# Moving two small softmax steps from VectorE to GpSimd in the attention stage of an attention and mixture-of-experts kernel

## The chip, the cores and the metric

The kernel runs on one core of a Trainium2 chip. The time is the device time of one execution in microseconds (us): the median of three runs is 686.33 us, the lowest 684.86 and the highest 687.82. A core has four compute engines that work side by side and wait for one another by semaphores: TensorE (PE in the profile; its weight loads are PEld), VectorE (DVE), ScalarE (ACT) and GpSimd (POOL). SyncE (SP) only issues transfers here.

## The reference

Three layers follow one another: causal attention with a decay (4 batches, 8 heads, 576 positions, 64 channels), a soft mixture of 8 experts with 4 slots each, and a second mixture of 4 experts that is weighted by given probabilities. The change is in the softmaxes of the middle layer, which the kernel computes during attention.

```python
def _attn_ref(q, k, v, f):
    scores = scale * np.matmul(q, k.transpose(0, 1, 3, 2))
    log_f = np.log(np.clip(f, 0.0001, 1.0))
    cum = np.cumsum(log_f, axis=-1)
    decay = cum[:, :, :, None] - cum[:, :, None, :]
    scores = np.where(causal, -1000000000.0, scores + decay)
    ...softmax over the last axis...
    return np.matmul(attn, v)

def _moe_ref(x, phi, w1, w2):           # x: 2304 tokens x 512
    logits = x @ phi                    # 2304 x 32
    d = np.exp(logits - logits.max(0, keepdims=True))
    d /= d.sum(0, keepdims=True) + 1e-09        # dispatch: over the tokens
    slot_input = (d.T @ x).reshape(E, S_per_e, D)
    for e in range(E):
        slot_out[e] = np.maximum(slot_input[e] @ w1[e], 0.0) @ w2[e]
    c = np.exp(logits - logits.max(1, keepdims=True))
    c /= c.sum(1, keepdims=True) + 1e-09        # combine: over the 32 slots
    return c @ slot_out

def _moe2_ref(x, domain_probs, w1, w2):
    p = domain_probs / (domain_probs.sum(-1, keepdims=True) + 1e-09)
    for e in range(E):
        out += p[:, e:e + 1] * (np.maximum(x @ w1[e], 0.0) @ w2[e])
    return out
```

## The kernel before

**The attention loop.** The 32 (batch, head) combinations are worked in 16 pairs of heads. A pair has seven steps (`STEPS`, `NS` = 7): step 3 does the last block of queries for both heads together, the other six do one block of 128 queries (or two) of one head. In each step `scores` multiplies queries with keys on TensorE; `soft` takes the masked minimum on VectorE (L198, a custom instruction with a second one that reads its result `nm`) and the exponential on ScalarE (L202); two steps later `transposes` turns the exponentials around on TensorE (L249, L258), and ScalarE or VectorE copies them out of PSUM (L168 and L170 are the two arms of the helper `copy`). `av_a` and `av_b` (L276, L288) multiply with the values for the pair before.

**The split of the operands.** Scores use a high and a low part of q and k. `split_a` and `split_b` make them for the heads of the next pair: ScalarE casts q (L168 CAST), GpSimd scales q (L180, which waits until TensorE has read the old operand) and subtracts (L179, which waits for the cast), VectorE casts k (L170 CAST), and GpSimd subtracts (L190). These are GpSimd's main work in attention.

**What is done once in a batch.** When the four pairs of a batch are done, the logits of its 576 tokens lie in `lg`, 128 partitions by 5 chunks by 32 slots. During the first pair of the next batch, `after_tr` calls three pieces of softmax work. At step 2 `dlog` turns the logits (PE L371, L372), finds the dispatch maximum of the tokens so far (`nm`, L377) and takes the exponentials (`dt`, and `al`, the factor for the sums so far, L382). At step 3 `csoft1` takes each token's maximum (`cm`, L350), subtracts it (`ce`, L352) and takes the exponential on ScalarE (L355). At step 4 `dnat` turns `dt` back (L395), `dsum` updates the running maximum `mm[:, 0:1]` and the running sum `ssum` (L387 to L389), and `csoft2` normalizes the combine weights (L360 to L363). At step 6 `sadd` adds to the slot inputs `s_sb` on TensorE (L406, L412) and VectorE (L415); after it `logits` and its PE lines L322 and L324 follow. This happens three times, for batches 0, 1 and 2; the last batch is finished by other code after the loop, which calls `csoft1` too, and there L352 is on GpSimd already.

**What sets the order.** In the loop TensorE's order is fixed by hand (`manual_schedule` for PE). The order on the other engines is found by the framework's scheduler when the kernel is built; each engine then works off its list in order, and each instruction waits for what it needs. Both kernels can be listed engine by engine.

Of the kernel before, what the change touches and what calls it, by code (L numbers as in the profile page):

```python
# [13 lines left out]
ALU = mybir.AluOpType  # L14
# [3 lines left out]
B, H, S, D = 4, 8, 576, 64  # L18
# [16 lines left out]
def soft_moe_kernel(tc, a, out):  # L35
    nc = tc.nc
    pe, dve, act, pool, sp = nc.tensor, nc.vector, nc.scalar, nc.gpsimd, nc.sync
# [10 lines left out]
    with ExitStack() as top:  # L48
# [101 lines left out]
        mm = tl.tile([128, 5], F32, name="mm")  # L150
        warm, ssum = mm[0:1, 4:5], mm[:, 3:4]
# [115 lines left out]
        lt, av, ot, xn, lb = {}, {}, {}, {}, {}  # L267
# [79 lines left out]
        def csoft1(b):  # L347
            lg = lb[b]["lg"]
            cm = sm.tile([128, 5], F32, tag="cm", bufs=1, name=f"cm_{b}")
            dve.tensor_reduce(cm, lg, axis=AX.X, op=ALU.max)  # L350
            ce = wk.tile([128, 5, 32], F32, tag="ce", bufs=1, name=f"ce_{b}")
            (pool if b == B - 1 else dve).tensor_tensor(ce, lg, cm[:, :, None].to_broadcast([128, 5, 32]), op=ALU.subtract)  # L352
            lb[b]["ce"] = ce
            if b < B - 1:
                act.activation(ce, ce, AF.Exp)  # L355
# [28 lines left out]

        def dsum(b):
            al, ds = lb[b]["al"], lb[b]["ds"]
            dve.tensor_scalar(mm[:, 0:1], lb[b]["nm"], -1.0, None, op0=ALU.mult)  # L387
            dve.scalar_tensor_tensor(ssum, ssum, al, ds[:, 0:1], op0=ALU.mult, op1=ALU.add)
            dve.tensor_tensor(ssum, ssum, ds[:, 1:2], op=ALU.add)  # L389

        def dnat(b):
            dt = lb[b]["dt"]
# [52 lines left out]
        def after_tr(g):  # L445
            pr, st = divmod(g, NS)
            pr -= 1
            b = pr // NP - 1
            if st == 5 and 0 <= pr < LASTP and not (pr and pr % NP == 0):
                nat(pr)  # L450
            if st == 0 and pr > 1 and (pr - 1) % NP == 0:
                logits(pr - 1)
            if pr > 0 and pr % NP == 0:
                if st == 2:
                    dlog(b)
                elif st == 3:
                    csoft1(b)
                elif st == 4:
                    dnat(b)
                    dsum(b)  # L460
                    csoft2(b)
# [84 lines left out]
        with tc.manual_schedule(engines={E.PE, E.Activation, E.DVE}):  # L546
# [20 lines left out]
            lg = lb[B - 1]["lg"]  # L567
# [3 lines left out]
            lm = scr[:, 130:162]  # L571
            dve.tensor_reduce(lm, lg[:, 0:4].rearrange("p c s -> p s c"), axis=AX.X, op=ALU.max)
            csoft1(B - 1)
            pe.transpose(mt[:, 128:192], lg[:64, 4], ident[:64, :64])
            pe.transpose(mt[:, 0:128], lm, ident)
# [6 lines left out]
            nm = sm.tile([128, 1], F32, tag="dm", bufs=1, name="dm_e")  # L582
            dve.tensor_reduce(nm[:32], mm[:32, 0:2], axis=AX.X, op=ALU.max, negate=True)
            ds = sm.tile([128, 2], F32, tag="ds", bufs=1, name="ds_e")
            dt = wk.tile([128, S], F32, tag="dt", name="dt_e")
            act.activation(dt[:32], tr, AF.Exp, bias=nm[:32], accum_out=ds[:32, 0:1])
            al = sm.tile([128, 1], F32, tag="al", bufs=1, name="al_e")
# [18 lines left out]
            ce = lb[B - 1]["ce"]  # L606
# [166 lines left out]
        for e in range(E1 - 2):  # L773
# [18 lines left out]
            if e == 5:  # L792
# [14 lines left out]
                for jq in range(4):  # L807
                    for i in range(2):
# [3 lines left out]
                                           op1=ALU.mult)  # L812
# [419 lines left out]
```

## Time and profile before

| quantity | before |
|---|---|
| median of three runs | 686.33 us (684.86 to 687.82) |
| the profiled execution, its own time | 686.2 us |
| its span | 684.4 us |
| PE busy | 664.2 us (97% of the span) |
| DVE busy | 505.4 us (74%) |
| POOL busy | 415.2 us (61%) |
| ACT busy | 342.2 us (50%) |

The span is the time from the first to the last instruction that the profile holds; 1.8 us of the execution lie around it. Attention takes about the first 228 us. The three stretches in which the once-a-batch work runs begin at about 73, 126 and 178 us; they look alike to a few hundredths of a microsecond, so the rows below are of the first, and the others are named where it matters. The mean of a group over the whole span says little about them.

### The profile page before, as it was taken

Reading aid. Unit: us, or ns where it says so; the run is one execution under the profiler, and the core shown is the slowest. Engines: PE = TensorE matmul, PEld = TensorE weight load, DVE = VectorE, ACT = ScalarE, POOL = GpSimd, SP = SyncE. Lnnn points to the kernel's source line nnn. Section 1 sums busy time; section 2 is a strip of 40 time slices with the busy share of each in tenths; the row PEclk is TensorE's granted clock in tenths of the full one; section 3 lists DMA queues with packets and bytes.
Section 4 is the critical chain, followed back from the end, with each engine's and each line's share of the span. In section 5 each row is a group of like instructions: output and inputs, shape, how many; then the busy total and the mean of one; then the engine's idle time right before and its main releaser. Section 6 shows DMA issues by size and latency. Waiting matters only on the chain.

```text
span 684.4 us, 15289 instructions
## 1 busy us (share of the span) xinstructions
PE 664.2 (97%) x5642; PEld 584.1 (85%) x5642; DVE 505.4 (74%) x1370; ACT 342.2 (50%) x817; POOL 415.2 (61%) x377
## 2 busy tenths in 40 slices
PE   6999999999999999999999999999999999999997
PEld 3777677677677545999999999999999999999997
DVE  7888987998996302976777976777976777977764
ACT  4767666766664103633455534455534355544441
POOL 5677656657652126953589934589934589935442
PEclk8899999999999999999999999999999999999999
DMA  6587778723325896031100112100212100001111
GB/s 191 174 263 246 240 228 270 225 76 108 107 56 216 333 417 258 1 124 56 70 1 1 73 53 68 57 1 1 85 41 82 43 2 1 32 33 62 47 47 62
DMA packets 27138, 76.15 MB, mean 111 GB/s; under 512 B 3772, under 2 KB 4156, under 8 KB 27064
## 3 DMA queue, kind: packets, MB, share of 16 engines
q1 hardware_dynamic: 27064, 75.18, 32.1%
q8 instruction: 45, 0.74, 0.5%
q14 instruction: 29, 0.24, 0.1%
HBM read 70.31 MB, written 4.72 MB: 110 GB/s over the span
## 4 chain that ended last, share of the span: by engine, by line
PE 88%; DVE 8%; issue 2%; ACT 1%; SPq 1%; DMA 1%; POOL 0%; DVEq 0%; ACTq 0%
PE R L1022 27%; PE Q L1022 13%; PE P L1022 7%; PE avb L276 5%; PE pt L258 5%; PE two L835 5%; PE d L1042 3%; PE sc L228 3%; PE sc L212 3%; PE sc L227 2%; PE two L731 2%; PE pl L324 2%; PE ava L288 2%; PE so_ps L755 2%; PE pt L249 2%
## 5 line engine op out<-in xcount | busy, mean ns | idle before, releaser
L901 POOL TENSOR_TENSOR s<-S,s 128x512 fp32r<-128x512 f32 x136 | 174.3, 1316 | 137.8 <-ACT s L897 137.8
L897 ACT CAST s<-S 128x512 fp32r<-128x512 f32 x136 | 75.0, 619 | 86.1 <-DVE S L893 75.9
L202 ACT ACTIVATE p<-p,nm 128x256 f32<-128x256 f32 (+2 forms) x144 | 83.4, 580 | 49.8 <-DVE nm L198 49.3
L1022 PE MATMUL R<-wh_T,s 128*128 128x256 f32 x544 | 87.2, 282 | 0.5 <-DVE acc L1005 0.4
L1005 DVE SCALAR_TENSOR_TENSOR acc<-R,dpn,acc 128x256 f32<-128x256 f32 x115 | 55.5, 482 | 38.9 <-PE R L1022 37.1
L867 ACT ACTIVATE a<-two 128x256 f32<-128x256 f32 x68 | 26.1, 383 | 98.8 <-PE two L835 95.2
L1022 PEld LDWEIGHTS R<-wh_T,s 128*128 128x128 f32 x544 | 74.4, 190 | 1.0 <-ACT a L876 1.0
L198 DVE CUSTOM_DVE_ANT_0 p<-sc,maskb 128x256 f32<-128x256 f32 (+2 forms) x144 | 66.1, 488 | 3.9 <-PE sc L212 0.9
L893 DVE SCALAR_TENSOR_TENSOR S<-two,S 128x256 f32<-128x256 f32 x136 | 57.1, 420 | 3.0 <-POOL s L901 0.2
L893 DVE SCALAR_TENSOR_TENSOR S<-two,a 128x256 f32<-128x256 f32 x136 | 56.3, 414 | 0.0
L179 POOL TENSOR_TENSOR opd<-raw,opd 64x576 fp32r<-64x576 f32 x30 | 44.6, 1486 | 13.7 <-ACT opd L168 12.3
L258 PE MATMUL pt<-ident,p 128*128 128x128 f32 x288 | 47.7, 285 | 4.6 <-ACT ptb L168 2.5
L190 POOL TENSOR_TENSOR opd<-raw,opd 64x576 fp32r<-64x576 f32 x31 | 44.0, 1421 | 10.8 <-DVE opd L170 9.5
L258 PEld LDWEIGHTS pt<-ident,p 128*128 128x128 f32 x288 | 31.3, 143 | 21.9 <-issue 16.4
L227 PE MATMUL sc<-opd 128*128 128x256 f32 (+3 forms) x128 | 47.5, 381 | 1.0 <-POOL opd L179 1.0
L883 DVE SCALAR_TENSOR_TENSOR q<-two,q 128x512 fp32r<-128x512 f32 x68 | 46.3, 680 | 0.0
L835 PE MATMUL two<-c4t,gs 128*128 128x256 f32 x288 | 45.8, 282 | 0.3 <-ACT gs L168 0.3
L180 POOL TENSOR_SCALAR opd<-raw 64x576 fp32r<-64x576 f32 x30 | 20.5, 683 | 39.9 <-PE sc L228 17.9
L276 PE MATMUL avb<-ptb,v 128*64 128x192 f32 (+3 forms) x384 | 43.9, 348 | 0.4
L1022 PE MATMUL R<-wh_T,q 128*128 128x256 f32 x272 | 44.1, 285 | 0.0
L1022 PE MATMUL Q<-wh_B,s 128*128 128x256 f32 x272 | 43.6, 283 | 0.0
L1022 PE MATMUL R<-wh_B,a 128*128 128x256 f32 x272 | 43.6, 282 | 0.0
(245 smaller groups left out, 1699.6 us busy)
## 6 DMA issues: line engine op xcount, KB each, us to landing
w<-in_w SPq DMA_DIRECT2D x50, 512.0 KB, 5.0
ring<-in_m SPq DMA_DIRECT2D x28, 512.0 KB, 6.1
raw<-in_k SPq DMA_DIRECT2D x64, 144.0 KB, 2.9
v<-in_v SPq DMA_DIRECT2D x16, 320.0 KB, 5.2
out<-acc SPq DMA_DIRECT2D x18, 256.0 KB, 2.0
raw<-in_q SPq DMA_DIRECT2D x15, 288.0 KB, 4.3
ring<-in_w SPq DMA_DIRECT2D x8, 512.0 KB, 4.6
w_opd<-in_w SPq DMA_DIRECT2D x4, 512.0 KB, 5.2
```

The source lines that it names most:

```text
L198: dve.tensor_tensor_reduce(out=pt_in[j][:, k0:k0 + n], in0=sc, in1=maskb[:, m0:m0 + n], scale=-SCALE, scalar=nm, op0=ALU.add, op1=ALU.min, ...
L202: act.activation(p, p, AF.Exp, bias=nm, scale=-1.0, accum_out=sums)
L227: pe.matmul(o, lhsT=qa[hh][:, qs], rhs=ka[hh][:, 0:n], start=True, stop=False)
L258: pe.transpose(t[:, i, :], pt_in[j][:, 128 * i:128 * i + 128], ident)
L276: pe.matmul(t[64 * hh:64 * hh + 64, q0:q1], lhsT=v_raw[pr][:kk, i, 64 * hh:64 * hh + 64], rhs=ptb[2 * pr + hh][:kk, b0:b0 + q1 - q0], star ...
L835: pe.matmul(t[:, j, k], lhsT=gs[e][:, 128 * fc:128 * fc + 128], rhs=c4t[:, nb * BLK:nb * BLK + BLK])
L883: dve.scalar_tensor_tensor(o[:, 1], i, 0.0, f32(o[:, 0]), op0=ALU.max, op1=ALU.subtract)
L893: dve.scalar_tensor_tensor(sv[m, name][:, c], half[m, h][:, :, k, 128 * t:128 * t + 128], 0.0, other, op0=ALU.max, op1=op)
L897: act.copy(tile_of(m, name)[:, 0], sv[m, name])
L901: (eng or pool).tensor_tensor(o[:, 1], sv[m, name], f32(o[:, 0]), op=ALU.subtract)
L1005: dve.scalar_tensor_tensor(o, t, pcol, o, op0=ALU.mult, op1=ALU.add)
L1022: pe.matmul(t, lhsT=a[:, c, :], rhs=w[:, c, :], start=first and x == 0 and c == 0, stop=x == 2 and c == 3, skip_group_check=True)
```

## The change

`csoft1` puts the subtraction of the maximum (L352) on GpSimd for every batch, where before that was so for the last batch only. `dsum` is written anew on GpSimd: the scaling of `nm` stays one instruction, and the update of `ssum`, a scalar_tensor_tensor and a tensor_tensor before, becomes three tensor_tensor instructions, each of one element in a partition. What is computed is the same.

```diff
@@ csoft1
             dve.tensor_reduce(cm, lg, axis=AX.X, op=ALU.max)
             ce = wk.tile([128, 5, 32], F32, tag="ce", bufs=1, name=f"ce_{b}")
-            (pool if b == B - 1 else dve).tensor_tensor(ce, lg, cm[:, :, None].to_broadcast([128, 5, 32]), op=ALU.subtract)
+            pool.tensor_tensor(ce, lg, cm[:, :, None].to_broadcast([128, 5, 32]), op=ALU.subtract)
@@ dsum
             al, ds = lb[b]["al"], lb[b]["ds"]
-            dve.tensor_scalar(mm[:, 0:1], lb[b]["nm"], -1.0, None, op0=ALU.mult)
-            dve.scalar_tensor_tensor(ssum, ssum, al, ds[:, 0:1], op0=ALU.mult, op1=ALU.add)
-            dve.tensor_tensor(ssum, ssum, ds[:, 1:2], op=ALU.add)
+            pool.tensor_scalar(mm[:, 0:1], lb[b]["nm"], -1.0, 1.0, op0=ALU.mult, op1=ALU.mult)
+            for x, op in ((al, ALU.mult), (ds[:, 0:1], ALU.add), (ds[:, 1:2], ALU.add)):
+                pool.tensor_tensor(ssum, ssum, x, op=op)
```

On VectorE the place is the first pair after batch 0, from the maximum `cm` to the copies of the transposed exponentials; a minus marks what the list of before has and that of the change has not. `sc`, `p` and `nm` are scores, exponentials and minima of attention, `dm` is the dispatch maximum, `ptb` a copy of transposed exponentials, and `mm` holds `ssum` in one of its columns.

```order
 L350 TENSOR_REDUCE cm_1102<-lg_448 128x5
 L170 CAST opd_91<-raw 128x576
-L352 TENSOR_TENSOR ce_1104<-lg_448,cm_1102 128x160
 L198 ISA p_126,nm_4_1_1077<-sc_1_1065,maskb,nm_4_0_1075 128x192
 L198 ISA nm_4_1_1077 128x1
-L387 TENSOR_SCALAR mm<-dm_1057 128x1
-L388 SCALAR_TENSOR_TENSOR mm<-mm,al_1062,ds_1047 128x1
-L389 TENSOR_TENSOR mm<-mm,ds_1047 128x1
 L170 COPY ptb_1096<-pt_1095 128x4x128
 L219 COPY rs<-r_5_1074 64x1 x2
```

Four instructions have left VectorE's list, two stretches of it close up, and nothing else on it changes its place.

On GpSimd at the same place the list of before reads as follows; `opd` are the operands of the scores, and the names end in the number of a tile.

```order
L343 TENSOR_SCALAR l_0_974<-lg_448 128x640
L190 TENSOR_TENSOR opd_92<-raw,opd_92 64x576
L180 TENSOR_SCALAR opd_91<-raw 64x576
L179 TENSOR_TENSOR opd_91<-raw,opd_91 64x576
L190 TENSOR_TENSOR opd_91<-raw,opd_91 64x576
L180 TENSOR_SCALAR opd_92<-raw 64x576
L179 TENSOR_TENSOR opd_92<-raw,opd_92 64x576
```

The list of the change, from the same instruction on:

```order
L343 TENSOR_SCALAR l_0_974<-lg_448 128x640
L190 TENSOR_TENSOR opd_92<-raw,opd_92 64x576
L180 TENSOR_SCALAR opd_91<-raw 64x576
L179 TENSOR_TENSOR opd_91<-raw,opd_91 64x576
L352 TENSOR_TENSOR ce_1104<-lg_448,cm_1102 128x160
L190 TENSOR_TENSOR opd_91<-raw,opd_91 64x576
L387 TENSOR_SCALAR mm<-dm_1057 128x1
L389 TENSOR_TENSOR mm<-mm,al_1062 128x1
L389 TENSOR_TENSOR mm<-mm,ds_1047 128x1 x2
L180 TENSOR_SCALAR opd_92<-raw 64x576
L179 TENSOR_TENSOR opd_92<-raw,opd_92 64x576
```

L352 now stands between an L179 and an L190, and the four small instructions stand between that L190 and the next L180. The lists of TensorE, ScalarE and SyncE keep their order.

## Rows read from the trace of the kernel before

**Rows 1.** The page: busy time by engine, and engines in the last chain.
```profile
PE 664.2 (97%) x5642; PEld 584.1 (85%) x5642; DVE 505.4 (74%) x1370; ACT 342.2 (50%) x817; POOL 415.2 (61%) x377
...
PE 88%; DVE 8%; issue 2%; ACT 1%; SPq 1%; DMA 1%; POOL 0%; DVEq 0%; ACTq 0%
```
**Rows 2.** The chain of waits: start us, us, what (three batches, then the first).
```profile
77.23 1.45 DVE ce L352
...
129.78 1.45 DVE ce L352
...
182.33 1.45 DVE ce L352
...
83.76 1.24 DVE cn L363
```
**Rows 3.** One stretch: its bounds and length, busy us by engine, clock, DMA.
```profile
73.00:90.00 17.00, 15.44 (x128) 10.69 (x126) 16.25 (x55) 9.88 (x31) 9.63 (x9) 1.00 0.73 248
```
**Rows 4.** Timeline, DVE, 77 to 84 us: start, us, instruction [idle before <-releaser].
```profile
77.15 1.53 DVE L352 TENSOR_TENSOR ce<-lg,cm 128x160 f32<-128x160 f32 x1
...
78.94 0.14 DVE L387 TENSOR_SCALAR mm<-dm 128x1 f32<-128x1 f32 x1
79.01 0.99 DVE L388 SCALAR_TENSOR_TENSOR mm<-mm,al,ds 128x1 f32<-128x1 f32 x1
...
80.11 0.68 DVE L170 COPY ptb<-pt 128x512 f32<-128x512 f32 x1
...
81.04 0.42 DVE L198 CUSTOM_DVE_ANT_0 p<-sc,maskb 128x256 f32<-128x256 f32 x1
...
83.68 1.44 DVE L363 TENSOR_TENSOR cn<-ce,cs 128x160 f32<-128x160 f32 x1
```
**Rows 5.** Timeline, POOL, 76 to 85 us.
```profile
76.97 1.53 POOL L179 TENSOR_TENSOR opd<-raw,opd 64x576 fp32r<-64x576 f32 x1
78.58 1.41 POOL L190 TENSOR_TENSOR opd<-raw,opd 64x576 fp32r<-64x576 f32 x1
82.02 0.67 POOL L180 TENSOR_SCALAR opd<-raw 64x576 fp32r<-64x576 f32 x1 [2.03 <-PE sc L228]
83.53 1.41 POOL L179 TENSOR_TENSOR opd<-raw,opd 64x576 fp32r<-64x576 f32 x1 [0.84 <-ACT opd L168]
```
**Rows 6.** Timeline, ACT, 77 to 84 us.
```profile
77.70 0.29 ACT L382 ACTIVATE al<-mm,dm 128x1 f32<-128x1 f32 x1
79.11 0.78 ACT L202 ACTIVATE p<-p,nm 128x576 f32<-128x576 f32 x1 [1.12 <-DVE nm L198]
...
80.19 0.34 ACT L355 ACTIVATE ce<-ce 128x160 f32<-128x160 f32 x1
...
81.51 0.51 ACT L202 ACTIVATE p<-p,nm 128x256 f32<-128x256 f32 x1 [0.61 <-DVE nm L198]
...
82.40 0.35 ACT L168 COPY ptb<-pt 128x256 f32<-128x256 f32 x1
82.78 0.67 ACT L168 CAST opd<-raw 64x576 fp32r<-64x576 f32 x1
```
**Rows 7.** Timeline, PE, 77 to 86 us.
```profile
77.62 0.66 PE L258 MATMUL pt<-ident,p 128*128 128x128 f32 x4
...
80.94 0.63 PE L258 MATMUL pt<-ident,p 128*128 128x128 f32 x4 [0.83 <-ACT ptb L168]
...
85.84 0.33 PE L322 MATMUL pl<-ident,ot 128*128 128x128 f32 x1 [0.48 <-DVE s_sb L415]
```
**Rows 8.** Groups by line and form, POOL: busy us, mean ns | idle before.
```profile
L722 POOL TENSOR_TENSOR wl_T<-T,wh_T 128x1024 fp32r<-128x1024 f32 x1 | 3.4, 3384 | 0.0
...
L810 POOL TENSOR_SCALAR sel<-i 32x64 fp32r<-32x64 f32 x8 | 1.8, 237 | 0.2
...
L352 POOL TENSOR_TENSOR ce<-lg,cm 128x160 f32<-128x160 f32 x1 | 0.5, 453 | 7.1 <-DVE cm L350 7.1
...
L159 POOL MEMSET mm<- 128x1 f32 x1 | 0.1, 98 | 0.1
```

## The prediction

> **What bounds the kernel now.** I read the page first. TensorE is busy 97% of the span and holds 88% of the chain that ended last; VectorE holds 8% of that chain [rows 1]. So the question is whether the moved instructions lie in those 8%. The chain of waits in order of time answers it: the subtraction L352 stands in it three times, once for each batch that has it on VectorE, with 1.45 us each [rows 2]. The stretch around the first, 73 to 90 us, says the same from another side: VectorE is busy 16.25 of 17 us there, more than TensorE with 15.44, and TensorE's granted clock is 1.00, the full 2.4 GHz [rows 3]. For some ten microseconds in each of three batches VectorE is what everything else waits for, and there work taken off VectorE is worth something.
>
> Then the timelines of VectorE and GpSimd, held against each other. L352 handles 160 elements and takes 1.53 us on VectorE from 77.15 to 78.68, while GpSimd's L179 runs from 76.97 to 78.50. L388 handles one element and takes 0.99 us, from 79.01 to 80.00, while GpSimd's L190 runs to 79.99. L363, again 160 elements, takes 1.44 us, from 83.68 to 85.12, while GpSimd's second L179 runs to 84.94 [rows 4, 5]. Three times a short VectorE instruction with two operands in SBUF ends when a GpSimd instruction ends, within 0.2 us. L387, with one operand, takes 0.14 us in the middle of L190 [rows 4, 5]. So the long ones are stalls: VectorE is held until GpSimd's running instruction is over. What the change takes off VectorE is mainly two such stalls; the third, on L363, stays.
>
> **The change part by part.** *Removed from VectorE, for each batch:* 1.45 us of L352 in the chain [rows 2], and the stretch from the start of L387 at 78.94 to that of the next L170 at 80.11, 1.17 us [rows 4]. Together 2.62 us, or 7.9 us in three batches, is what VectorE gets back and the upper bound of the gain.
>
> *Added to GpSimd, for each batch:* L352 there takes 0.453 us in the last batch [rows 8], and I take that. The four small instructions have no row of their own. From below they cost as much as a fill of 128x1, 98 ns each, so 0.39 us; from above one tensor_scalar like L810 with 237 ns and three tensor_tensor like L352 with 453 ns, together 1.60 us [rows 8]. Nothing excludes the low end, and one element a partition is nearest to the fill, so I take 0.6 us. Below nothing they can't be: they are four instructions more. Their cover is GpSimd's idle time of 2.03 us before L180 [rows 5]. Queued behind them are L190, L180 and L179, and the transfers that SP issues once these have read the raw operands; the even head's operand that L190 writes by 79.99 (some 0.5 us later now) is first used by the next pair's scores, behind the rest of this pair.
>
> *The new wait:* ScalarE's L355 now needs GpSimd's L352. That one follows L179, which ends at 78.50, so it runs from 78.58 to about 79.03. ScalarE gets there as follows: it is done with L382 at 77.99, and the exponential L202 behind it waited until 79.11 for the minimum behind L352 [rows 6]; now it starts at about 78.0, and L355, 1.08 us behind it (80.19 less 79.11), at 79.08. That is 0.05 us after GpSimd is done, so the wait costs nothing, and has no slack: behind L355 stand the copy of ptb and all of ScalarE's list.
>
> *What is late next.* VectorE's L170, at 80.11 before, no longer has anything in front of it but its data: TensorE's transposes run from 77.62 to 78.28 [rows 7], so it starts at about 78.35. TensorE had waited 0.83 us until 80.94 [rows 7]; its data and its buffer are now there by 79, so it goes on at 80.11, without a gap. VectorE's L198 stood 0.93 us behind L170 (81.04 less 80.11) and comes at 79.3 now; ScalarE's L202, 0.47 us later, at 79.75 instead of 81.51, and the copy of ptb, 0.89 us behind that (82.40 less 81.51), would be ready at 80.64 [rows 4, 6]. But it copies what TensorE transposes from 80.11 on, for 0.63 us; with 0.1 us for the semaphore it starts at 80.84, and the cast 0.38 us behind it (82.78 less 82.40) at 81.22. So the cast comes 1.56 us earlier, and it is the head of what follows: L179 waits for the cast [rows 5], L363 is held by L179 [rows 4, 5], L415 follows L363, and TensorE's L322 waited for L415 until 85.84 [rows 7]. All four move by 1.56 us. GpSimd's L180 doesn't stand in the way: it follows TensorE, which moves by 0.83, so it may start at 81.19, and GpSimd's list before it ends at about 79.99 + 0.53 (L352 and the 0.08 us from one instruction to the next, 78.58 less 78.50) + 0.6 = 81.1. With 0.67 us of its own it is done at 81.9, as the cast is.
>
> L363 stood 1.28 us behind ScalarE's copy of ptb (83.68 less 82.40), by way of VectorE's own copy from the same transposes, and L179 1.13 us (83.53 less 82.40) [rows 4 to 6]. Both hang on that copy, so L179 starts at 81.97 and L363 at 82.12; it is held again, and VectorE's third stall stays.
>
> *Sum.* 3 x 1.56 = 4.7 us. After L322 TensorE's list has no large gap in attention, and the chain after attention is TensorE's, whose weights are issued as buffers come free; so I let the gain reach the end. The profiled execution then takes 686.2 - 4.7 = 681.5 us, span 679.7; its own time is 0.1 us under the median of the runs shown, so I forecast 681.5 for the median as well.
>
> **The rivals.**
>
> *L363 escapes its stall (679.1 us).* By the sum L179 starts only 0.15 us ahead of L363. If VectorE is first, GpSimd waits instead, L363 loses most of its 1.24 us in the chain [rows 2], say 0.8, and the gain is 2.36 us a batch, 7.1 in all. Against it: the 0.15 us are those of before, and nothing in the sum shortens them unless VectorE, with less in its list, closes up behind the copy. The Trainium skill, "SBUF — State Buffer", section "SBUF: two separate sides", says that the shared ports of VectorE and GpSimd go whole to whichever instruction starts first. The three ends above agree for GpSimd being first; by that rule a VectorE that is first would win, which no row here shows.
>
> *GpSimd becomes late (684.2 us).* With the small instructions at their upper end of 1.60 us, GpSimd's list before L180 ends at 82.12, 0.93 us after TensorE would let it start, and L179 starts at 82.87, 0.9 us behind the sum. L363, L415 and L322 lose that again: 0.66 us a batch, 2.0 in all. For it: tensor_tensor on GpSimd has no short row in this trace. Against it: the fill with 98 ns.
>
> *The work only changes places (686.2 us).* GpSimd holds VectorE up with what it got, and nothing is won. It would need VectorE instructions with two SBUF operands while L352 and the small ones run on GpSimd, 78.6 to 81.1; VectorE's list has none there. The Trainium skill, "Perfetto Trace Analysis", section "Optimizing Scalar/DVE Operations", warns that moving operations between VectorE and GpSimd might not help, since they share a port. Here the stalls [rows 4, 5] show the sharing, and the direction of the move is what decides.
>
> *Slower: ScalarE waits for GpSimd (691.6 us).* One place: L355 behind GpSimd's L352. Before, L355 started at 80.19 [rows 6]; GpSimd can start L352 at 78.58, so from 1.6 us of L352 on, ScalarE's list is later than before, and TensorE's transposes with it. If L352 took as long as the longest tensor_tensor in the trace, 3.38 us [rows 8], it would end at 81.96, and each batch would lose 1.8 us: 5.4 us more. Against it stands L352's own row with 0.453 us; but in that stretch VectorE and GpSimd had less to do beside it.
>
> **How the numbers follow.** Half a percent, 3.4 us, is about what a measurement of this kernel can tell from no change: faster means under 682.9, slower over 689.8. The forecast, with its own range of 680.3 to 682.8, has 0.60. L363 escaping has 0.13, GpSimd late 0.15, only changing places 0.07, slower 0.05. Faster are the first two, 0.73; within half a percent the next two, 0.22; slower 0.05. The range for 8 in 10 leaves out the last two cases and the far ends of the second and third: 679.0 to 684.3.
>
> **What would show it right or wrong.** In the changed profile the first stretch should have: no VectorE instruction over 0.7 us between the cast of k and L363; GpSimd's L352 near 0.45 us, and the four small ones together under 1 us; ScalarE's L202 with 576 elements right behind L382; no gap on TensorE before the transposes of 80.94; L363 still near 1.4 us; and the distance from TensorE's first L212 of that pair to the next pair's shorter by about 1.6 us. The chain of waits should have no L352. If L355 waits for POOL, or L180 starts later than TensorE allows, GpSimd's additions are dearer than I take them. If all of this is there and the total is not 3 to 6 us down, the gain is given back later, at the end of attention or where the expert weights arrive, and the forecast's last step is wrong.

## The result and the profile after

The changed kernel takes 678.88 us (median of 4 runs, 678.61 to 681.61), the kernel before on the same chip 686.04 us (4 runs, 684.86 to 687.82). The ratio is 0.9907, 95% interval 0.9885 to 0.9929: about 7 us less, where 4.7 were forecast. Applied to the 686.33 us from which the forecast started, the ratio gives 679.9 us: inside the range of 679.0 to 684.3, at its lower end, and below the forecast's own 680.3 to 682.8. The bare median of 678.88 lies 0.1 us under the range. Both are nearest to the rival "L363 escapes its stall" (679.1). The profiled execution took 679.08 us, its span 677.3.

The page after, busy time by engine and the engines in the last chain, answers to [rows 1]:

```profile
PE 660.2 (97%) x5642; PEld 583.2 (86%) x5642; DVE 493.9 (73%) x1358; ACT 341.7 (50%) x817; POOL 418.4 (62%) x392
...
PE 91%; DVE 4%; issue 2%; ACT 1%; SPq 1%; DMA 1%; POOL 0%; ACTq 0%; DVEq 0%
```

VectorE's part of the chain has fallen from 8% to 4%; neither L352 nor L363 stands in it any more, and from 75 to 90 us it is TensorE's without a break.

Two stretches of the kernel after (bounds and length, busy us by engine with instructions, granted clock, DMA): the one of [rows 3], and the first pair from its first L212 to the next pair's.

```profile
73.00:90.00 17.00, 17.00 (x147) 12.44 (x145) 14.41 (x57) 11.33 (x35) 10.87 (x15) 1.00 0.82 261
74.96:88.67 13.71, 13.71 (x119) 10.02 (x118) 11.91 (x48) 9.79 (x30) 8.94 (x13) 1.00 0.78 248
```

The same pair in the kernel before:

```profile
74.89:90.89 16.00, 14.44 (x119) 9.96 (x118) 15.46 (x52) 9.35 (x29) 7.75 (x8) 1.00 0.68 221
```

The same 119 matmuls take 13.71 us where they took 16.00, and TensorE has no idle time left among them. The pair lasts 13.71 us in each of the three batches, 16.00, 15.99 and 15.98 before: about 3 x 2.29 = 6.9 us, which is nearly the whole difference of the two profiled executions (686.2 less 679.08, 7.1). The gain reaches the end. Executions of one kernel lie some 2 to 7 us apart, so below I compare this pair's length beside the medians; it repeats to 0.02 us except where the text says otherwise.

VectorE's timeline after (start, us, instruction), which answers to [rows 4]:

```profile
78.38 0.69 DVE L170 COPY ptb<-pt 128x512 f32<-128x512 f32 x1 [0.75 <-PE pt L258]
...
79.32 0.42 DVE L198 CUSTOM_DVE_ANT_0 p<-sc,maskb 128x256 f32<-128x256 f32 x1
...
81.96 0.31 DVE L363 TENSOR_TENSOR cn<-ce,cs 128x160 f32<-128x160 f32 x1
82.37 0.75 DVE L415 SCALAR_TENSOR_TENSOR s_sb<-s_sb,al,sa 128x512 f32<-128x512 f32 x1
```

GpSimd's, which answers to [rows 5]:

```profile
77.03 1.53 POOL L179 TENSOR_TENSOR opd<-raw,opd 64x576 fp32r<-64x576 f32 x1
78.64 0.46 POOL L352 TENSOR_TENSOR ce<-lg,cm 128x160 f32<-128x160 f32 x1
79.06 1.41 POOL L190 TENSOR_TENSOR opd<-raw,opd 64x576 fp32r<-64x576 f32 x1
80.44 0.19 POOL L387 TENSOR_SCALAR mm<-dm 128x1 f32<-128x1 f32 x1
80.59 0.18 POOL L389 TENSOR_TENSOR mm<-mm,al 128x1 f32<-128x1 f32 x1
80.85 0.46 POOL L389 TENSOR_TENSOR mm<-mm,ds 128x1 f32<-128x1 f32 x2
81.40 0.67 POOL L180 TENSOR_SCALAR opd<-raw 64x576 fp32r<-64x576 f32 x1
82.03 1.52 POOL L179 TENSOR_TENSOR opd<-raw,opd 64x576 fp32r<-64x576 f32 x1
```

L363 starts at 81.96 and takes 0.31 us; the second L179 starts at 82.03. Before, L179 was first, by 0.15 us, and L363 took 1.44. The four small instructions fill GpSimd from 80.44 to 81.40, and L180 follows them without a wait.

ScalarE's timeline after, which answers to [rows 6]:

```profile
77.95 0.77 ACT L202 ACTIVATE p<-p,nm 128x576 f32<-128x576 f32 x1
...
79.13 0.34 ACT L355 ACTIVATE ce<-ce 128x160 f32<-128x160 f32 x1
...
80.68 0.35 ACT L168 COPY ptb<-pt 128x256 f32<-128x256 f32 x1
81.05 0.67 ACT L168 CAST opd<-raw 64x576 fp32r<-64x576 f32 x1
```

And TensorE's, which answers to [rows 7]:

```profile
80.01 0.60 PE L258 MATMUL pt<-ident,p 128*128 128x128 f32 x4
...
84.04 0.27 PE L322 MATMUL pl<-ident,ot 128*128 128x128 f32 x1
```

None of these six rows shows a wait in front of it: not L355 for GpSimd's L352, which ends at 79.10, nor L258 and L322, which had 0.83 and 0.48 us.

A shorter wait is gone behind them. TensorE's L276 writes `avb` into one of two PSUM tiles that are used in turn; by the kernel's order it is the one that `pl` held, and VectorE's L337 is the last to read `pl`. Before, then after:

```profile
88.95 0.27 DVE L337 TENSOR_TENSOR xn<-pl,ri 64x128 f32<-64x128 f32 x1
89.37 1.28 PE L276 MATMUL avb<-ptb,v 128*64 128x192 f32 x12
...
86.29 0.27 DVE L337 TENSOR_TENSOR xn<-pl,ri 64x128 f32<-64x128 f32 x1
87.20 1.23 PE L276 MATMUL avb<-ptb,v 128*64 128x192 f32 x12
```

Before, L276 starts 0.15 us after L337 ends and 1.00 us behind TensorE's L288; after, L337 has ended 0.64 us earlier, and L276 follows L288 by 0.70 us.

### The profile page after: what moved, and what is told of

It is laid out like the page before. It is cut to its first block, busy times and chain, and to the rows that moved or that the text cites. A ratio compares the mean times of both kernels' runs of the same rounds, so it can differ in the third digit from the quotient of the medians.

```text
span 677.3 us, 15304 instructions
## 1 busy us (share of the span) xinstructions
PE 660.2 (97%) x5642; PEld 583.2 (86%) x5642; DVE 493.9 (73%) x1358; ACT 341.7 (50%) x817; POOL 418.4 (62%) x392
## 4 chain that ended last, share of the span: by engine, by line
PE 91%; DVE 4%; issue 2%; ACT 1%; SPq 1%; DMA 1%; POOL 0%; ACTq 0%; DVEq 0%
PE R L1022 27%; PE Q L1022 13%; PE P L1022 7%; PE avb L276 6%; PE pt L258 5%; PE two L835 5%; PE d L1042 3%; PE sc L212 3%; PE sc L228 3%; PE sc L227 3%; PE two L731 2%; PE pl L324 2%; PE ava L288 2%; PE pt L249 2%; PE so_ps L755 2%
## 5 line engine op out<-in xcount | busy, mean ns | idle before, releaser
L179 POOL TENSOR_TENSOR opd<-raw,opd 64x576 fp32r<-64x576 f32 x30 | 44.7, 1490 | 11.1 <-ACT opd L168 9.7
L258 PE MATMUL pt<-ident,p 128*128 128x128 f32 x288 | 47.2, 282 | 2.5 <-DVE ptb L170 0.8
L190 POOL TENSOR_TENSOR opd<-raw,opd 64x576 fp32r<-64x576 f32 x31 | 44.1, 1423 | 6.7 <-DVE opd L170 5.7
L258 PEld LDWEIGHTS pt<-ident,p 128*128 128x128 f32 x288 | 31.1, 141 | 18.6 <-issue 14.5
L276 PE MATMUL avb<-ptb,v 128*64 128x192 f32 (+3 forms) x384 | 43.8, 347 | 0.0
L1022 PE MATMUL R<-wl_T,s 128*128 128x256 f32 x272 | 43.5, 282 | 0.0
```

What stands on the lines that cost most here:

```text
L258: pe.transpose(t[:, i, :], pt_in[j][:, 128 * i:128 * i + 128], ident)
L276: pe.matmul(t[64 * hh:64 * hh + 64, q0:q1], lhsT=v_raw[pr][:kk, i, 64 * hh:64 * hh + 64], rhs=ptb[2 * pr + hh][:kk, b0:b0 + q1 - q0], star ...
L1022: pe.matmul(t, lhsT=a[:, c, :], rhs=w[:, c, :], start=first and x == 0 and c == 0, stop=x == 2 and c == 3, skip_group_check=True)
```

## The experiments

The working theory after the result: VectorE is held by GpSimd at three places, the change removes two of these, and the third goes because the small instructions delay L179 past L363. Each comparison below has runs of the kernel before on the same chip; "measured" gives the median (lowest to highest), the median of the kernel before, and the ratio of the two with its 95% interval.

**One half of the change each.** The kernel before with L352 alone on GpSimd:

```diff
-            (pool if b == B - 1 else dve).tensor_tensor(ce, lg, ..., op=ALU.subtract)
+            pool.tensor_tensor(ce, lg, ..., op=ALU.subtract)
```

> Only the subtraction L352 moves to GpSimd; the update of the running sum stays on VectorE. Theory (a VectorE instruction with two SBUF operands waits for GpSimd's running one, and in the changed kernel L363 came free because GpSimd's second L179 began at 82.03, behind L363 at 81.96): here GpSimd has no small instructions, so L179 begins at about 81.8 and L363 is held again, 1.2 to 1.4 us. L388 is held to the end of the first L179, near 78.6. A gain of 1.4 to 1.9 us a batch: 680.5 to 682. Rival (each moved piece is worth its own time in the chain, 1.45 and 1.17 us a batch, whatever stands beside it): 686.0 - 4.4 = 681.7, and L363 as short as in the changed kernel, 0.31 us.

Measured: 681.53 us against 685.69, ratio 0.9945 (0.9924 to 0.9965); the pair lasts 14.51 us in every batch, 1.49 less than before. Two groups by line (shortest, median and longest of the three, in ns) and GpSimd's two instructions:

```profile
L363 DVE TENSOR_TENSOR cn<-ce,cs x3: 1106/1115/1116, 81.4 to 183.7; 128x160 f32<-128x160 f32 x3
...
L388 DVE SCALAR_TENSOR_TENSOR mm<-mm,al,ds x3: 422/422/422, 77.0 to 179.3; 128x1 f32<-128x1 f32 x3
...
79.93 0.67 POOL L180 TENSOR_SCALAR opd<-raw 64x576 fp32r<-64x576 f32 x1 [0.64 <-PE sc L228]
80.92 1.41 POOL L179 TENSOR_TENSOR opd<-raw,opd 64x576 fp32r<-64x576 f32 x1 [0.32 <-ACT opd L168]
```

Without the small instructions GpSimd still waits for TensorE before L180, L179 comes first, and L363 is held: from 81.41 to 82.52, where L179 ends at 82.33. L388 takes 0.42 us instead of 0.99. The total fits the theory and the rival alike; L363 at 1.11 us and not 0.31 decides for the theory.

The kernel before with the new `dsum` alone:

```diff
-            dve.tensor_scalar(mm[:, 0:1], lb[b]["nm"], -1.0, None, op0=ALU.mult)
-            dve.scalar_tensor_tensor(ssum, ssum, al, ds[:, 0:1], ...)
-            dve.tensor_tensor(ssum, ssum, ds[:, 1:2], op=ALU.add)
+            pool.tensor_scalar(mm[:, 0:1], lb[b]["nm"], -1.0, 1.0, ...)
+            for x, op in ((al, ALU.mult), (ds[:, 0:1], ALU.add), (ds[:, 1:2], ALU.add)):
+                pool.tensor_tensor(ssum, ssum, x, op=op)
```

> Only the update of the running sum moves to GpSimd; L352 stays on VectorE. Theory: L352 is still held until GpSimd's L179 ends, so the exponential of 576 elements on ScalarE still starts near 79.1 and the cast of q only 0.5 to 0.8 us earlier than before; about 2 us over three batches, 684, with L352 at 1.5 us. L363 depends on which is first again. Rival (each piece worth its own time): 686.0 - 3.5 = 682.5.

Measured: 683.35 us against 685.69, ratio 0.9967 (0.9952 to 0.9981); the pair lasts 15.31 us, 0.69 less. The groups by line:

```profile
L352 DVE TENSOR_TENSOR ce<-lg,cm x3: 1529/1529/1530, 76.7 to 180.0; 128x160 f32<-128x160 f32 x3
...
L363 DVE TENSOR_TENSOR cn<-ce,cs x3: 1440/1442/1444, 82.5 to 185.9; 128x160 f32<-128x160 f32 x3
```

Both are held as before. The total lies between the theory's 684 and the rival's 682.5 and decides nothing; the rows do. So neither half alone frees L363; together they do, though the two gains, 1.49 and 0.69, already add up to 2.18 of the 2.29 us.

**The small instructions taken away.** If they cost only time, the change without them should be quicker; if they decide who is first, slower. In the changed kernel `dsum` does nothing:

```diff
-            pool.tensor_scalar(mm[:, 0:1], lb[b]["nm"], -1.0, 1.0, ...)
-            for x, op in ((al, ALU.mult), (ds[:, 0:1], ALU.add), (ds[:, 1:2], ALU.add)):
-                pool.tensor_tensor(ssum, ssum, x, op=op)
+            return
```

> The changed kernel without the update of the running maximum and the running sum on any engine (these two stay at their first values); everything else as changed. It does less work than the changed kernel. Theory of the race: without the four small instructions GpSimd's L180 begins at 81.1 and its L179 at about 81.8, ahead of L363 at 81.96; L363 is held until L179 ends, 1.2 to 1.4 us instead of 0.31, and the kernel is SLOWER than the changed one by about 1 us (0.3 to 0.4 us a batch): 679.6 to 680.5. Rival (GpSimd's extra instructions are a cost, or nothing): the same as the changed kernel or less, 678 to 679, with L363 at 0.31 us.

> The changed kernel without the update of the running maximum and sum on any engine, once more, now on one chip with the changed kernel itself, since the first time its trace held L363 for 1.44 us and a pair took 0.48 us longer, but the medians of two sessions can't be set against each other so finely. Race theory: 1.0 to 1.5 us slower than the changed kernel beside it, and 14.2 us from L212 to L212 against 13.7. Rival (the small instructions cost GpSimd time that matters): faster than it.

Measured: 680.13 us (679.2 to 684.22) against 685.69, ratio 0.9921 (0.9897 to 0.9945); on another chip 681.49 (679.14 to 683.47) against 686.8, ratio 0.9916 (0.9888 to 0.9944). The pair lasts 14.19 to 14.21 us in all batches of both. GpSimd and, below it, VectorE in the second:

```profile
79.27 0.67 POOL L180 TENSOR_SCALAR opd<-raw 64x576 fp32r<-64x576 f32 x1 [0.64 <-PE sc L228]
79.96 1.40 POOL L179 TENSOR_TENSOR opd<-raw,opd 64x576 fp32r<-64x576 f32 x1
...
80.11 1.44 DVE L363 TENSOR_TENSOR cn<-ce,cs 128x160 f32<-128x160 f32 x1
```

Less work, and 0.49 us longer a pair than with it. This pair's first L212 is at 73.11, 1.85 us before that of the changed kernel (74.96). Moved by that, L363 stands at 81.96 in both; L179 stands at 81.81 here and at 82.03 there. So 0.22 us on GpSimd decide about 1.44 or 0.31 us on VectorE. The medians point the same way (681.49 beside 679.2, below), but their spreads overlap; it is the traces that show it.

The changed kernel again on the chip of that second run, and once more on the one of the last runs below:

> The changed kernel as it is, as the measure for the three others of this set. All theories: 679 us, L363 at 0.31 us, 13.7 us from L212 to L212.

> The changed kernel as it is, as the measure for the two others of this set: 679 us.

Measured: 679.2 us (678.55 to 680.83) against 686.8, ratio 0.9886 (0.9861 to 0.9911); and 679.03 (677.28 to 680.31) against 685.77, ratio 0.989 (0.9864 to 0.9917). Of nine pairs in the three profiles eight last 13.71 or 13.72 us and one 13.90. In all nine L363 starts 0.07 to 0.10 us before L179 and takes 0.31 or 0.32 us.

**More small instructions.** The changed kernel with four additions more at the same place, which change the sum:

```diff
-            for x, op in ((al, ALU.mult), (ds[:, 0:1], ALU.add), (ds[:, 1:2], ALU.add)):
+            for x, op in ((al, ALU.mult), (ds[:, 0:1], ALU.add), (ds[:, 1:2], ALU.add)) + ((ds[:, 0:1], ALU.add),) * 4:
```

> The changed kernel with four more instructions of one element on GpSimd in the update of the sum (the first part of the new sums is added four times more, so the sum is another number). Theory: GpSimd's list has room; its L180 starts 1.0 to 1.1 us later, near 82.5, L179 near 83.1, far behind L363, which stays at 0.31 us; L179's result is needed only by the next pair's fourth step. No change: within 0.5 us of the changed kernel, 13.7 us from L212 to L212. Rival (late GpSimd work is paid by the operands of the scores): 1 us a batch slower, 682.

Measured: 680.98 us (678.38 to 683.73) against 686.8, ratio 0.9904 (0.987 to 0.9937). GpSimd, and below it VectorE:

```profile
80.01 1.73 POOL L389 TENSOR_TENSOR mm<-mm,ds 128x1 f32<-128x1 f32 x6
81.83 0.67 POOL L180 TENSOR_SCALAR opd<-raw 64x576 fp32r<-64x576 f32 x1
82.47 1.40 POOL L179 TENSOR_TENSOR opd<-raw,opd 64x576 fp32r<-64x576 f32 x1
...
81.11 0.31 DVE L363 TENSOR_TENSOR cn<-ce,cs 128x160 f32<-128x160 f32 x1
```

L179 is now 1.36 us behind L363, and the pair lasts 13.71, 13.76 and 13.71: GpSimd has that much room, and being later costs nothing in this pair. The total was to stay within 0.5 us of the changed kernel on the same chip (679.2); the median is 1.8 us above it, but the spreads overlap, so the totals decide nothing here.

**The race taken out.** The changed kernel with L363 on GpSimd as well, behind L179:

```diff
-            dve.tensor_tensor(cn[:, b], ce, ..., op=ALU.mult)
+            pool.tensor_tensor(cn[:, b], ce, ..., op=ALU.mult)
```

> The changed kernel, and L363 on GpSimd too for batches 0 to 2. Theory: TensorE has no gap left in this stretch, its pair takes 13.7 us, the 11.9 of an ordinary pair and 1.8 of extra work; so nothing more is to be had: within 0.5 us of the changed kernel, 678.5 to 679.5. Rival (VectorE still bounds the stretch): another 0.3 to 0.4 us a batch, 677.8.

> The changed kernel with L363 on GpSimd too, once more, on one chip with the changed kernel. Theory: TensorE has no gap left in this stretch; the same time within 0.5 us, 13.7 us from L212 to L212. Rival (VectorE's 0.31 us of L363 still counts): 0.9 us faster.

Measured: 678.4 us (676.55 to 679.44) against 685.69, ratio 0.9889 (0.9869 to 0.9909); again 679.09 (678.26 to 679.79) against 685.77, ratio 0.989 (0.9866 to 0.9914), beside 679.03 of the changed kernel on the same chip. The pair is the same, 13.71. GpSimd in the second:

```profile
81.02 1.42 POOL L179 TENSOR_TENSOR opd<-raw,opd 64x576 fp32r<-64x576 f32 x1
82.52 0.46 POOL L363 TENSOR_TENSOR cn<-ce,cs 128x160 f32<-128x160 f32 x1
```

There is nothing more to be had here: once L363 isn't held, TensorE sets the pair. This form doesn't hang on 0.07 us, but it isn't faster.

**L363 alone on GpSimd**, the same line in the kernel before:

> The kernel before, with only L363 on GpSimd for batches 0 to 2: the third stall alone is taken away, the two that the change takes away stay. Theory: L352 and L388 are held as before (1.5 and 1.0 us), TensorE keeps its gap of 0.83 us before the transposes and loses the 0.48 us before L322 and about 0.3 us behind it: 15.2 us from L212 to L212 instead of 16.0, 2 to 2.4 us in all, 683.5 to 684.5. Rival (the third stall stands in the chain with 1.24 us and is worth that): 3.7 us, 682.3.

Measured: 682.14 us (679.82 to 685.46) against 685.77, ratio 0.9945 (0.9926 to 0.9964), 3.6 us, more than the theory's 2 to 2.4. The pair lasts 14.19, 14.19 and 14.93 us in the profiled execution. GpSimd, then VectorE's L352 in the first and in the third batch:

```profile
75.35 0.91 POOL L180 TENSOR_SCALAR opd<-raw 64x576 fp32r<-64x576 f32 x1 [1.78 <-DMA raw<-in_q]
76.34 1.41 POOL L179 TENSOR_TENSOR opd<-raw,opd 64x576 fp32r<-64x576 f32 x1
...
75.65 0.79 DVE L352 TENSOR_TENSOR ce<-lg,cm 128x160 f32<-128x160 f32 x1
...
176.88 1.54 DVE L352 TENSOR_TENSOR ce<-lg,cm 128x160 f32<-128x160 f32 x1
```

In two batches q's transfer landed late and GpSimd's first L179 came behind L352. L352 then ends at 76.44, behind L180 (76.26) and not behind L179 (77.75), so that stall was cut from 1.54 to 0.79 us. In the third, undisturbed, the pair is 1.05 us shorter: this is what L363 alone is worth in the kernel before. On top of the change it is worth 0.49 (above): there the wait of 0.48 us before L322 has mostly gone with the other two stalls. How often the transfer is late in the other runs, and so how the 3.6 us are made up, stays open.

**What is held.** Is it two operands in SBUF, as I had read it from L387? The kernel before, with L352 written in batches 0 to 2 as five instructions with one such tensor and a scalar for each partition:

```diff
+            [dve.tensor_scalar(ce[:, c], lg[:, c], cm[:, c:c + 1], None, op0=ALU.subtract) for c in range(5)] if b < B - 1 else ...
```

> The kernel before, with L352 on VectorE as five tensor_scalar instructions, one for each chunk, whose subtrahend is a scalar a partition: one SBUF operand instead of two. Theory (two SBUF operands are what is held): each of the five is under 0.2 us, none is held by the L179 that runs beside them, and the exponential of 576 elements starts at about 78.0 instead of 79.1. L388 is held only to the end of L179. About 681.5 to 682.5 if L389 slips in before L190 as it did in the run with L352 alone on GpSimd; 685 if it is held until L190 ends. Rival (VectorE is held at any SBUF to SBUF instruction while GpSimd runs, or the subtraction with its repeated operand is slow by itself): the first of the five, or all together, takes 1.2 us or more, and nothing is won: 685.5 to 686.5.

Measured: 690.11 us (687.33 to 693.92) against 686.8, ratio 1.0038 (1.0015 to 1.0062): 0.4% slower, above both forecasts. GpSimd, then VectorE:

```profile
75.84 1.52 POOL L179 TENSOR_TENSOR opd<-raw,opd 64x576 fp32r<-64x576 f32 x1
77.43 1.41 POOL L190 TENSOR_TENSOR opd<-raw,opd 64x576 fp32r<-64x576 f32 x1
82.10 0.67 POOL L180 TENSOR_SCALAR opd<-raw 64x576 fp32r<-64x576 f32 x1 [3.26 <-PE sc L228]
...
76.01 1.39 DVE L352 TENSOR_SCALAR ce<-lg,cm 128x32 f32<-128x32 f32 x1
...
77.64 1.67 DVE L352 TENSOR_SCALAR ce<-lg,cm 128x32 f32<-128x32 f32 x4
...
82.23 0.56 DVE L361 TENSOR_SCALAR cs<-cs 128x5 f32<-128x5 f32 x1
```

The first of the five ends at 77.40, with L179 (77.36), and the next, 1.23 us long, at 78.87, with L190 (78.84). So the theory of two operands falls: these instructions read one tensor and are held all the same; a free one takes 0.23 us (the median of the 15). The scalars for each partition lie in SBUF too, but a hold doesn't need them: L361, 128x5 with a constant, is held behind L180 for 0.56 us, against 0.16 in the other batches, and takes 0.50 in all three of the kernel with L352 alone on GpSimd. TensorE and its stretches then show the price:

```profile
80.44 0.93 PE L258 MATMUL pt<-ident,p 128*128 128x128 f32 x4 [1.47 <-DVE ptb L170]
...
81.94 1.94 PE L406 MATMUL sa<-xn,dnn 128*32 128x512 f32 x8
...
80.00:82.00 2.00, 1.56 (x10) 1.16 (x14) 1.96 (x11) 1.04 (x6) 0.00 (x0) 0.66 0.71 246
82.00:84.00 2.00, 2.00 (x13) 0.34 (x16) 2.00 (x8) 1.95 (x5) 1.65 (x2) 0.50 0.19 38
...
187.59 0.63 PE L258 MATMUL pt<-ident,p 128*128 128x128 f32 x4 [1.48 <-DVE ptb L170]
...
187.00:190.00 3.00, 2.30 (x22) 1.03 (x22) 2.96 (x16) 2.02 (x7) 0.67 (x1) 1.00 0.18 55
```

The gap before L258 grew from 0.83 to 1.47 us, and behind it the granted clock is 0.50, its level of 1.2 GHz; L406's eight matmuls take 1.94 us, 1.06 in the changed kernel. The pair lasts 16.93 us, 0.93 more than before. The other two batches have the same gap, 1.47 and 1.48 us. In the second the clock falls too (0.56 from 135 to 137 us) and the pair lasts 17.14; in the third (the last two rows) the clock stays at 1.00 and it lasts 16.65. So the five instructions with their holds cost 0.67 us without the clock, and the gap's length alone doesn't settle whether the clock falls.

## Why the prediction was right and where it was wrong

- **The number: inside the range by a rival.** The forecast of 681.5 us with its own range missed. The wide range holds the result because it was drawn to take in "L363 escapes its stall", which had 0.13; as to the forecast's own path, that is luck.
- **The bound, and the two stalls: right.** The theory that GpSimd holds L352 and L388, and that taking them off VectorE shortens each pair, is shown by the two halves: 1.49 and 0.69 us. That only instructions with two operands in SBUF are held was wrong ("What is held", above); the sum didn't use it.
- **L352 on GpSimd and ScalarE behind it: right.** 0.46 us for 0.453; L355 at 79.13 for 79.08, without a wait. The slower case didn't occur.
- **TensorE without a gap: right, and 0.23 us too late.** I let L258 follow the end of L228's row (79.71 + 0.40 = 80.11). Matmul rows overlap: L228 starts at 79.78 after, L258 0.23 us behind it. That is 0.17 of the 0.23 us (L258 stands 5.05 us behind the pair's first L212, forecast 5.22); the rest is the step from L258 to the copy, 0.67 us where I had 0.63 + 0.1. So ScalarE's copy of ptb, counted from the pair's first L212, comes at 5.72 instead of 7.51 us, 1.79 earlier where I had 1.56. The experiment without the small instructions has the held L363 of the forecast, and gains that: 16.00 less 14.20, 1.80 a pair, 5.4 in all and not 4.7.
- **The step that failed: "so I take 0.6 us."** The four small instructions hold GpSimd from 80.44 to 81.40, 0.96 us: 0.18 to 0.19 each, and the gaps between them. The sum gave GpSimd 0.09 us of slack before L180 and L179 0.15 us of lead over L363: from about 0.6 + 0.09 + 0.15 = 0.84 us on, VectorE is first. My bounds of 0.39 to 1.60 us held that point, and I had worked out what lies beyond it as a loss ("GpSimd becomes late").
- **So "it is held again, and VectorE's third stall stays" fell.** L363 was 1.28 us behind the copy of ptb, as forecast (81.96 less 80.68), but L179 was 1.35 behind it and not 1.13. VectorE was first, and GpSimd was late by an amount that nobody waited for. The Trainium skill, "SBUF — State Buffer", section "SBUF: two separate sides", gives the shared ports to whichever starts first, for the whole instruction; the trace agrees, 0.31 us against 1.44 by a lead of 0.07 us. GpSimd's L179, now second, takes 1.50 to 1.52 us, against 1.42 where L363 isn't on VectorE ("The race taken out").
- **The rival that came in: right in its sum, not in its parts.** It gave 2.36 us a pair, measured 2.29. The stall was to bring 0.8 of that; it brought 0.49 (14.20 less 13.71), of which 0.07 show at L322 (9.15 us behind the first L212 without the small instructions, 9.08 with them) and 0.42 behind it. From L322 to the next pair's first L212 it is 5.05 us in the kernel before and 4.63 after; I had taken this stretch as fixed, since no row of it shows a wait. But 0.30 of the 0.42 us lie between L288 and L276 (1.00 us before, 0.70 after). In all 15 profiled pairs of the kernel before, of the two halves and of the two runs without the small instructions, L276 starts 0.14 to 0.15 us after VectorE's L337 ends: VectorE, held at L363, is still late there, and TensorE waits for it.
- **"The work only changes places", and GpSimd's lateness as a loss: wrong here.** With four more small instructions L179 stands 8.36 us behind the pair's first L212, 1.29 later than in the changed kernel and later than the 7.98 of that rival, and the pair is the same.

## What to carry to other kernels

Where a short VectorE instruction ends whenever a GpSimd instruction does, its length is a wait, and it depends on which of the two starts first: before forecasting, work out both starts, and ask whether the bounds of an unknown cost lie on both sides of the point at which the order turns. If they do, the cases on its two sides are the forecast, and a delay of the other engine can be the gain. Compare a repeated stretch between two fixed instructions rather than totals: here it mostly repeats to 0.02 us, where totals spread over 2 to 7.

## What was not expected of the hardware

- One-element instructions on GpSimd take 0.18 to 0.19 us, twice the fill of [rows 8] and less than half of the 160-element subtraction.
- A VectorE tensor_scalar of 128x32 from one tensor was held for 1.39 us, one of 128x5 for 0.50 to 0.56; L387, 128x1, was not, at 0.14 [rows 4]. Where the line runs is open.
- An idle time of 1.47 us on TensorE was followed by the clock's lower level in two batches of the run with five instructions; in the third, after 1.48 us, the granted clock stayed at 1.00, as it did after 0.83 us in the kernel before [rows 3]. What decides it is open.
- When a transfer lands can decide which engine is first: L352 took 0.79 us where q was late and 1.54 where it was not.
